# Cosine attention with a mixer behind it: the last score chunks of two head pairs in one score tile

## The chip, the core and the metric

The kernel runs on one core of a Trainium2 chip. The metric is device time in microseconds (us), the median of several executions; lower is better. The engines are TensorE (PE, with its weight loads shown as PEld), VectorE (DVE), ScalarE (ACT), GpSimd (POOL) and SyncE (SP). Each takes its instructions in the order in which they stand in its own queue. A fill of one engine by another is guarded by semaphores.

## What is computed

Inputs q, k and v have 8 batches, 12 heads, 448 rows and 64 columns. Each head's rows of q and k are normalised, the scores are divided by tau (0.1), and softmax and the product with v follow. The heads side by side give x with 448 rows and 768 columns for each batch, and a mixer follows:

```python
q_n = q / (np.linalg.norm(q, axis=-1, keepdims=True) + 1e-06)
k_n = k / (np.linalg.norm(k, axis=-1, keepdims=True) + 1e-06)
scores = np.matmul(q_n, k_n.transpose(0, 1, 3, 2)) / tau
attn = softmax(scores)                      # max subtracted, 1e-9 in the sum
x = heads side by side of np.matmul(attn, v)
h = x.transpose(0, 2, 1) @ U @ V            # rank 32 over the 448 rows
u = x + h.transpose(0, 2, 1)
out = u + np.maximum(u @ w_ch1, 0.0) @ w_ch2   # 768 -> 3072 -> 768
```

## The kernel before

Two heads make a pair, so each batch has six pairs, and all batches together have 48. For a pair, the keys of each head are cut into chunks of 128, 128, 128 and 64. Scores are held transposed: keys on the partitions, 448 queries on the columns. Chunks 0 to 2 take one score tile each (`sc`, two banks, one bank for each head), filled by four matmuls on the four 64x64 quarters of TensorE's array. The last chunk has 64 keys from each of the two heads, so both fit into the 128 partitions of one bank: one full 128x128 matmul, whose stationary side has zeros where a head has no keys, fills the first half of a score tile. There are two score tiles (tag `ps_sc`), used in turn. An exponential on ScalarE moves each tile into SBUF: 896 columns for chunks 0 to 2 (into `E`, one buffer for even and one for odd pairs), 448 columns for the last chunk (into `E3`, which has room for the two pairs of a couple: 0 and 1, 2 and 3, 4 and 5).

The product with v for a pair runs in two halves of the query rows. Each half begins with two matmuls that take the last chunk's exponentials as weights (line 376), and twelve for the other chunks follow (line 383). The first half goes to the bank `av`, the second to `mp`. VectorE divides each half by its sum (lines 394 and 395).

For batch 0 the order of everything is written out by hand as a list of words, `ORDER` (line 630). A word is put on its engine's queue when its turn comes, so the list is the order on each engine. The words that matter, with n a pair's number:

- `Tn`: TensorE transposes pair n's normalised q and k (bank `ps_x`, line 300). `Ten`: VectorE moves them into SBUF as `qkT` (line 305).
- `Snc`: the scores of chunk c of pair n (line 331, and line 324 for c = 3). `exnc`: their exponential (line 356, and line 353 for c = 3).
- `Vnh`: the product with v, half h. `Xnh`: VectorE's division.
- `An`: the product with U (line 416), into columns of bank `mp`. `Acn`: its copy into SBUF. `XTn`: the transpose of the divided result into `ps_x` (line 430). `Hn`: the product with V, added to it (line 441). `Un`: the move to `u` (line 446).
- `sc4q`, `sc4k` and their like: the scaling of q and k by their norms on POOL (.p) or VectorE (.v). `sq`, `red`, `root`, `inv`: the norms' squares, sums, roots and inverses. `val`: the values' cast. `l5q` and the like: loads on SP's queue. `w`n: matmuls of the identity without use, in the beginning. `w1_`i: a part of the first weight matrix, loaded by POOL's queue.
- `Mfab`: matmuls a to b of block f of the mixer's first product (line 655), which come when batch 0's `u` is nearly complete. `Rf`: their ReLU.

After the list, a loop goes over the pairs of the later batches and lays the mixer's matmuls of the batch before (lines 513 and 540) between the attention's steps. The second weight matrix comes in four transfers (line 173), all issued by POOL after squares and loads that stand ahead of them in its queue. A ReLU of the mixer's first product goes to ScalarE (line 517) or VectorE (line 519) by a planner's estimate: the object `est` keeps a running time for TensorE, ScalarE and VectorE, each step adds its estimated duration, and the engine that would be done first gets the work. In batch 0, too, the steps add their durations to it.

From pair 14 on the last chunks of two pairs are already handled together by `step_S3` (line 335): four matmuls on 64x64 quarters, the first pair's into the bank `av`, the second's into the bank `up`, and two exponentials.

Of the kernel before, what the change touches and what calls it, by code (L numbers as in the profile page):

```python
# [9 lines left out]
FP = mybir.dt.float32  # L10
BF = mybir.dt.bfloat16
AF = mybir.ActivationFunctionType
# [10 lines left out]
def kernel(  # L23
# [17 lines left out]
    nc = tc.nc  # L41

    B, H, S, D = q.shape
# [11 lines left out]
    psum = ctx.enter_context(tc.tile_pool(name="psum", bufs=1, space=bass.MemoryType.PSUM))  # L55
# [54 lines left out]
    E, E3 = [], []  # L110
# [37 lines left out]
    def place_v(copy, rows):  # L148
        lo = V_raw[rows, 0:256].rearrange("r (p c) -> r c p", c=4)
        hi = V_raw[rows, 256:448].rearrange("r (p c) -> r c p", c=3)  # L150
        body = V_sb[rows, 0:384].rearrange("r (c p) -> r c p", p=128)
        copy(out=body[:, :, 0:64], in_=lo[:, 0:3, :])
        copy(out=body[:, :, 64:128], in_=hi)
        copy(out=V_sb[rows, 384:448], in_=lo[:, 3, :])

    def place_u():
        nc.scalar.copy(out=U_sb[:, :, 0:R], in_=U_raw)
# [9 lines left out]
    def load_w1(f0, f1):  # L167
        nc.gpsimd.dma_start(out=w1_sb[:, :, f0:f1],
                            in_=moe_w_ch1[:, f0:f1].rearrange("(c p) f -> p c f", p=128))
# [20 lines left out]
    def load(gi, what, *engs):  # L190
        b, p0, n = groups[gi]
        engs = list(engs) * 4
        h0, nh = 2 * p0, 2 * n
        s = gi % NST

        def src(x, hs, lo, hi, c):
            return x[b, hs, lo:hi, :].rearrange("h (p c) d -> p h (c d)", c=c)

        def dst(t, ps, hs, c):
            return t[ps, hs, 0:c, :].rearrange("p h c d -> p h (c d)")  # L200

        L, U2 = slice(0, 64), slice(64, 128)
        if what == "q":
            allh = slice(h0, h0 + nh)
            engs[0].dma_start(out=dst(qst[s], L, slice(0, nh), 4), in_=src(q, allh, 0, 256, 4))
            engs[1].dma_start(out=dst(qst[s], U2, slice(0, nh), 3), in_=src(q, allh, 256, 448, 3))
            return
        x, t = (k, kst[s]) if what == "k" else (v, vst[s])
        m = min(3, nh)
        ou, mi = slice(h0, h0 + nh, 3), slice(h0 + 1, h0 + m)  # L210
        engs[0].dma_start(out=dst(t, L, slice(0, nh, 3), 4), in_=src(x, ou, 0, 256, 4))
        engs[1].dma_start(out=dst(t, U2, slice(0, nh, 3), 3), in_=src(x, ou, 256, 448, 3))
        engs[2].dma_start(out=dst(t, L, slice(1, m), 3), in_=src(x, mi, 0, 192, 3))
        engs[3].dma_start(out=dst(t, U2, slice(1, m), 4), in_=src(x, mi, 192, 448, 4))
# [89 lines left out]
    def evict_T(b, p):  # L304
        nc.vector.tensor_copy(out=new_qkT(b, p).rearrange("p a b -> p (a b)"),
                              in_=tp_of.pop((b, p)).rearrange("p a b -> p (a b)"))
        est.dve(0.69)
# [24 lines left out]
                                 rhs=t[r, 0, 0:S], start=True, stop=True)  # L332
        est.pe(0.25)

    def step_S3(b, p):

        for i, (nm, tag) in enumerate((("av", "ps_av"), ("up", "ps_x"))):
            t = qkT[(b, p + i)]
            bank = psum.tile([128, 512], FP, name=nm, tag=tag, bufs=1)
            sc_of[(b, p + i, 3)] = bank.unsqueeze(1)  # L340
            for h in range(2):
                r, o = slice(64 * h, 64 * h + 64), 64 * (h ^ i)
                nc.tensor.matmul(out=bank[o:o + 64, 0:S], lhsT=t[r, 1, 384 + o:448 + o],  # L343
                                 rhs=t[r, 0, 0:S], start=True, stop=True)
        est.pe(0.19)
        for i in range(2):
            exp_S(b, p + i, 3)

    def exp_S(b, p, c):
        e = E[(b * NP + p) % 2]  # L350
        sc = sc_of.pop((b, p, c))
        if c == 3:
            nc.scalar.activation(out=last_of(b, p)[:, 0:S], in_=sc[:, 0, 0:S], func=AF.Exp)  # L353
            est.act(0.56)
        else:
            nc.scalar.activation(out=e[:, 2 * c:2 * c + 2, 0:S], in_=sc[:, :, 0:S], func=AF.Exp)  # L356
            est.act(0.93)
# [62 lines left out]
    def evict_A(b, p, copy):  # L420
        A_of[(b, p)] = A_sb[p % 2]
        copy(out=A_sb[p % 2][0:64, :], in_=av_of[(b, p, 1)][0:64, 384:512])
# [17 lines left out]
    def pe_H(b, p):  # L440
        nc.tensor.matmul(out=up_of[(b, p)], lhsT=A_of[(b, p)], rhs=V_sb,  # L441
                         start=False, stop=True, skip_group_check=True)
        est.pe(0.19)
# [143 lines left out]
    pairs = [(b, p) for b in range(B) for p in range(NP)]  # L587
# [33 lines left out]
    def Hs(n):  # L621
# [11 lines left out]
        red2q ex02 S03 w6 ex03 val0 l3v T1 root2 val1 l4q l4k l4v V00 Te1 plU inv2 S10 V01  # L633
        sc2q.v S11 ex10 w9 sc2k.v ex11 X01 sc3k.p S12 T2 X00 ex12 S13 sc3q.p Te2 A0 w3 sq3q.a plV.p
        Ac0.v S20 T3 sq3k.a w19 red3q ex13 red3k ex20 S21 V10 ex21 w1_0 V11 X10 S22 Te3 root3 val2
        l5q l5k l5v S23 ex22 inv3 XT0 H0 X11 sc4q.p ex23 S30 U0.v ex30 V20 sc4k.v S31 A1 ex31 S32
        X20 sc5q.p T4 Ac1.v ex32 Te4 V21 sc5k.p S33 X21 XT1 ex33 S40 val3 H1 ex40 A2 U1.v S41 V30
        Ac2.v ex41 S42 X30 T5 ex42 V31 Te5 S43 X31 ex43 S50 XT2 ex50 A3 S51 Ac3.v H2 V40 ex51 U2.v
        S52 X40 V41 w1_1 ex52 S53 X41 XT3 sq4q ex53 H3 A4 U3.a V50 Ac4.v XT4 X50 V51 sq4k H4 U4.a X51
        M004 A5 red4q Ac5.a XT5 M104 H5 U5.a M045 M145 M205 red4k root4 M056 M156 R0 inv4 sc6q.v sc6k.v  # L640
        R1 M256 M306 R2 R3
    """
# [2 lines left out]
    copies = {"a": nc.scalar.copy, "v": nc.vector.tensor_copy}  # L645
    QK = {"q": 0, "k": 1}

    opened = {}

    def pe_m1(fb, lo, hi):  # L650
        if lo == 0 and fb % 2 == 0:
            t = psum.tile([128, 2, 512], FP, name="sc", tag="ps_sc", bufs=2)
            opened[fb], opened[fb + 1] = t[:, 0, 0:S], t[:, 1, 0:S]
        for cc in range(lo, hi):
            nc.tensor.matmul(out=opened[fb], lhsT=w1_sb[:, cc, fb * 128:(fb + 1) * 128],
                             rhs=uE[:, cc, 0:S], start=(cc == 0), stop=(cc == CC - 1),
                             skip_group_check=True)

    def evict_m1(fb):
        nc.scalar.activation(out=relu[:, fb, 64:64 + S], in_=opened.pop(fb), func=AF.Relu)  # L660

    def word(w):
        w, _, eng = w.partition(".")
        if w.startswith("w1_"):
            i = int(w[3:])
            load_w1(768 * i, 768 * (i + 1))
        elif w[0] == "w":
            for _ in range(int(w[1:])):
                nc.tensor.matmul(out=spare[:, 0:128], lhsT=ident, rhs=ident, start=True, stop=True)
        elif w[0] == "l":  # L670
            load(int(w[1]), w[2], nc.sync)
        elif w == "plU":
            place_u()
        elif w == "plV":
            place_v({"a": nc.scalar.copy, "p": nc.gpsimd.tensor_copy}[eng], slice(0, R))
        elif w[0] == "M":
            pe_m1(int(w[1]), int(w[2]), int(w[3]))
        elif w[0] == "R":
            evict_m1(int(w[1]))
        elif w.startswith("sq"):  # L680
            preps[int(w[2])].square(QK[w[3]], eng == "a")
        elif w.startswith("red"):
            preps[int(w[3])].reduce(QK[w[4]])
        elif w.startswith("root"):
            preps[int(w[4])].root()
        elif w.startswith("inv"):
            preps[int(w[3])].invert()
        elif w.startswith("val"):
            preps[int(w[3])].values()
        elif w.startswith("sc"):  # L690
            gi, j = group_of[pairs[int(w[2])]]
            preps[gi].scale(QK[w[3]], j, {"v": V_, "p": P_}[eng])
        elif w.startswith("Te"):
            evict_T(*pairs[int(w[2])])
        elif w.startswith("ex"):
            exp_S(*pairs[int(w[2])], int(w[3]))
        elif w.startswith("XT"):
            pe_XT(*pairs[int(w[2])])
        elif w.startswith("Ac"):
            evict_A(*pairs[int(w[2])], copies[eng])  # L700
        else:
            at = pairs[int(w[1])]
            if w[0] == "T":
                pe_T(*at)
            elif w[0] == "S":
                pe_S(*at, int(w[2]))
            elif w[0] == "V":
                half = int(w[2])
                pe_V(*at, half, bank1 if half else
                     psum.tile([128, 512], FP, name="av", tag="ps_av", bufs=1))  # L710
            elif w[0] == "X":
                divide_V(*at, int(w[2]))
            elif w[0] == "A":
                pe_A(*at)
            elif w[0] == "H":
                pe_H(*at)
            else:
                assert w[0] == "U", w
                evict_H(*at, copies[eng])
# [78 lines left out]
    for n in range(NP, NPAIR + 1):  # L798
        b, p = pairs[n] if n < NPAIR else (B, 0)
# [116 lines left out]
```

## Time and profile before

| What | Value |
|---|---|
| median of 10 executions | 579.9 us (579.54 to 581.8) |
| the profiled execution's own time | 580.26 us |
| its span in the profile | 578.5 us |
| TensorE busy | 568.6 us, 98% of the span |
| ScalarE busy | 262.2 us, 45% |
| VectorE busy | 212.2 us, 37% |
| POOL busy | 213.8 us, 37% |
| granted TensorE clock | 1.00 |

The part that the change touches lies between about 24 and 36 us of the span. The table by stretches (start and end, length, then the busy time and number of instructions of PE, PEld, DVE, ACT and POOL, the granted clock, the DMA engines' busy share and GB/s) shows how the engines are taken up around it:

```profile
20.00:25.00 5.00, 4.60 (x76) 3.41 (x76) 4.40 (x9) 4.39 (x8) 2.85 (x5) 1.00 0.84 165
25.00:30.00 5.00, 4.93 (x75) 3.12 (x74) 4.12 (x12) 4.45 (x7) 3.53 (x3) 1.00 1.15 229
30.00:35.00 5.00, 4.90 (x83) 3.31 (x83) 3.55 (x11) 4.57 (x6) 2.77 (x3) 1.00 1.16 247
35.00:40.00 5.00, 4.84 (x74) 3.59 (x73) 3.92 (x10) 2.57 (x5) 2.85 (x2) 1.00 1.10 209
40.00:45.00 5.00, 5.00 (x28) 2.61 (x27) 4.10 (x7) 3.58 (x8) 1.85 (x2) 1.00 1.12 258
```

Here three engines are taken up nearly all the time between 20 and 35 us, TensorE, ScalarE and VectorE, and from 40 us on TensorE has no hole in a stretch. A matmul's busy time includes its way through the array, so that a matmul's length is more than what it holds the engine; the distance from its start to the next one's is what it holds.

### The profile page before, as it was taken

The numbers are of one execution on the slowest core, as the hardware profiler recorded it, in microseconds if no ns is written. First come the engines' busy times: TensorE is split into PE (matmuls) and PEld (weight loads), VectorE is DVE, ScalarE is ACT, GpSimd is POOL, SyncE is SP. The second block draws the span as 40 slices with busy tenths as digits, with TensorE's granted clock in tenths as the row PEclk, the third lists the DMA queues.
The fourth block names the chain that finished last, engine by engine and source line by source line (L and its number), as shares of the span: only waits on it lengthen the run. The fifth ranks groups of instructions, "written<-read, shape, count | busy, mean of one in ns | idle before, by whom it ended". The sixth has DMA issues, their size and how long they took to land.

```text
span 578.5 us, 12301 instructions
## 1 busy us (share of the span) xinstructions
PE 568.6 (98%) x5098; PEld 329.2 (57%) x5098; DVE 212.2 (37%) x460; ACT 262.2 (45%) x449; POOL 213.8 (37%) x202
## 2 busy tenths in 40 slices
PE   7899999999999999999999999999999999999997
PEld 6665566555565556555555555655565545555565
DVE  7874551433342334423324343432244332320011
ACT  5877544455333653446324555246443374214300
POOL 8756564715416236416055064253261420000000
PEclk9999999999999999999999999999999999999999
DMA  6899999696477376575365663773755640231022
GB/s 163 192 236 238 236 210 211 168 170 139 101 151 164 88 146 127 132 153 109 87 158 147 119 137 97 149 174 80 132 129 115 133 74 14 56 69 37 5 50 57
DMA packets 139881, 74.52 MB, mean 129 GB/s; under 512 B 86688, under 2 KB 139696, under 8 KB 139824
## 3 DMA queue, kind: packets, MB, share of 16 engines
q1 hardware_dynamic: 129568, 63.20, 50.7%
q0 software_dynamic: 9632, 10.01, 10.2%
q8 instruction: 40, 0.66, 0.5%
q10 hardware_dynamic: 624, 0.51, 0.3%
q14 instruction: 17, 0.14, 0.1%
HBM read 52.19 MB, written 11.01 MB: 109 GB/s over the span
## 4 chain that ended last, share of the span: by engine, by line
PE 86%; DMA 8%; DVE 1%; ACT 1%; SPq 1%; POOL 1%; issue 1%; ACTq 0%; DVEq 0%; POOLq 0%
PE mp L540 38%; PE mp L513 33%; DMA w_sb<-in_moe_w_ch_dram 5%; PE sc L331 5%; PE av L383 3%; PE up L383 2%; DMA qst<-in_q_dram 2%; DMA kst<-in_k_dram 2%; PE av L343 1%; PE av L376 1%; PE up L376 1%; PE up L469 1%; PE av L483 1%; ACT E L356 0%; DVE qk L268 0%
## 5 line engine op out<-in xcount | busy, mean ns | idle before, releaser
L540 PE MATMUL mp<-w_sb,relu 128*128 128x384 bf16 (+2 forms) x1368 | 233.6, 323 | 0.6 <-DMA w_sb<-in_moe_w_ch_dram 0.6
L540 PEld LDWEIGHTS <-relu 128*128 128x128 bf16 x1368 | 126.8, 98 | 89.0 <-issue 13.8
L513 PEld LDWEIGHTS <-w_sb 128*128 128x128 bf16 x1128 | 105.1, 98 | 99.1 <-issue 9.3
L517 ACT ACTIVATE relu<-mp 128x448 bf16<-128x448 f32 x163 | 88.7, 544 | 128.2 <-PE mp L513 128.2
L356 ACT ACTIVATE E<-sc 128x896 bf16<-128x896 f32 x144 | 125.2, 922 | 22.4 <-PE sc L331 21.4
L268 POOL TENSOR_TENSOR qk<-kst,inv 128x512 bf16<-128x512 f32 x43 | 45.9, 1068 | 234.6 <-DVE inv L262 227.5
L513 PE MATMUL mp<-uO,w_sb 128*128 128x448 bf16 x576 | 114.2, 352 | 0.0
L513 PE MATMUL mp<-uE,w_sb 128*128 128x448 bf16 x552 | 112.9, 353 | 0.0
L558 DVE TENSOR_TENSOR o_sb<-mp,ut 128x384 f32<-128x384 f32 (+2 forms) x51 | 28.0, 550 | 141.0 <-PE mp L540 141.0
L248 DVE TENSOR_REDUCE ss<-sq 128x16 f32<-128x1024 f32 (+1 forms) x50 | 57.7, 1165 | 1.6 <-POOL sq L243 0.8
L268 POOL TENSOR_TENSOR qk<-qst,inv 128x512 bf16<-128x512 f32 x44 | 47.4, 1077 | 1.3 <-PE up L441 1.3
L383 PEld LDWEIGHTS <-E 128*128 128x128 bf16 x1152 | 45.0, 97 | 0.0
L519 DVE TENSOR_SCALAR relu<-mp 128x448 bf16<-128x448 f32 x25 | 15.6, 625 | 76.3 <-PE mp L513 75.8
L331 PE MATMUL sc<-qkT 64*64 64x448 bf16 x576 | 42.3, 359 | 0.6 <-ACT E L356 0.3
L243 POOL TENSOR_TENSOR sq<-kst 128x1024 f32<-128x1024 f32 (+1 forms) x23 | 42.6, 1855 | 0.2
L243 POOL TENSOR_TENSOR sq<-qst 128x1024 f32<-128x1024 f32 x21 | 39.7, 1890 | 7.4 <-DMA qst<-in_q_dram 6.7
L276 POOL CAST v<-vst 128x1024 bf16<-128x1024 f32 (+1 forms) x25 | 25.1, 1004 | 15.6 <-DMA vst<-in_v_dram 13.1
L353 ACT ACTIVATE E<-av 128x448 bf16<-128x448 f32 x17 | 9.2, 540 | 47.3 <-PE up L343 47.3
L383 PE MATMUL av<-v,E 128*128 128x65 bf16 x624 | 28.0, 193 | 0.0
L394 DVE RECIPROCAL rd<-av 128x4 f32<-128x4 f32 x52 | 9.3, 179 | 47.3 <-PE av L383 47.3
L473 ACT CAST A_sb<-up 128x128 bf16<-128x128 f32 x19 | 5.0, 264 | 47.6 <-PE up L469 47.6
L376 PEld LDWEIGHTS <-E 128*128 128x128 bf16 x192 | 18.0, 98 | 14.5 <-issue 0.8
(97 smaller groups left out, 347.8 us busy)
## 6 DMA issues: line engine op xcount, KB each, us to landing
out_dram<-o_sb SPq DMA_DIRECT2D x108, 96.0 KB, 2.2
w_sb<-in_moe_w_ch_dram POOLq DMA_DIRECT2D x8, 1152.0 KB, 18.3
qst<-in_q_dram SPq DMA_DIRECT2D x23, 256.0 KB, 3.9
vst<-in_v_dram SPq DMA_DIRECT2D x46, 128.0 KB, 3.1
kst<-in_k_dram SPq DMA_DIRECT2D x44, 128.0 KB, 2.8
qst<-in_q_dram SPq DMA_DIRECT2D x23, 192.0 KB, 4.0
vst<-in_v_dram SPq DMA_DIRECT2D x46, 96.0 KB, 2.8
kst<-in_k_dram SPq DMA_DIRECT2D x44, 96.0 KB, 2.7
```

Source lines behind the costliest of these rows:

```text
L243: nc.gpsimd.tensor_mul(sq[:, 0:self.nh * 4, :], self.flat(t), self.flat(t))
L248: nc.vector.reduce_sum(self.ss[:, j, 0:self.nh * 4], self.sq[j][:, 0:self.nh * 4, :], axis=AX.X)
L268: eng.tensor_mul(qks[self.gi % 2][:, j, i, :, :, :], t[:, 2 * j:2 * j + 2, :, :].rearrange("p h c d -> p c h d"), iv.unsqueeze(3).to_broad ...
L276: nc.gpsimd.tensor_copy(out=self.flat(v65[self.s])[:, :, 0:D], in_=self.flat(vst[self.s]))
L331: nc.tensor.matmul(out=sc[o:o + 64, h, 0:S], lhsT=t[r, 1, c * 128 + o:c * 128 + o + 64], rhs=t[r, 0, 0:S], start=True, stop=True)
L356: nc.scalar.activation(out=e[:, 2 * c:2 * c + 2, 0:S], in_=sc[:, :, 0:S], func=AF.Exp)
L376: nc.tensor.matmul(out=av[:, i, :, :], lhsT=last_of(b, p)[:, ic * 128:(ic + 1) * 128], rhs=vv[:, 2 * j:2 * j + 2, 3, :], start=(i == 0), s ...
L383: nc.tensor.matmul(out=av[:, i, h, :], lhsT=e[:, 2 * c + h, ic * 128:(ic + 1) * 128], rhs=vv[:, 2 * j + h, c, :], start=False, stop=(i == ...
L513: nc.tensor.matmul(out=mp, lhsT=w1_sb[:, cc, f * 128:(f + 1) * 128], rhs=u[:, cc, 0:S], start=(cc == 0), stop=(cc == CC - 1))
L517: nc.scalar.activation(out=relu[:, f, o:o + S], in_=mp, func=AF.Relu)
L540: nc.tensor.matmul(out=mp, lhsT=relu[:, f, r0:r0 + 128], rhs=w2_sb[:, f, half * HC + c0:half * HC + c1], start=(f == 0), stop=(b > 0 and f ...
L558: nc.vector.tensor_add(o.rearrange("p (k d) -> p k d", d=128), mp.rearrange("p (k d) -> p k d", d=128), ut_of[(b, half)][:, c0 // 128:c1 / ...
```

## The change

In batch 0 the last chunks of pairs 2 and 3, and of pairs 4 and 5, are computed together. The words `S23`, `ex23`, `S33`, `ex33`, `S43`, `ex43`, `S53`, `ex53` go. The words `Q2`, `exQ2`, `Q4` and `exQ4` come. `Q`n takes one score tile, fills one bank for each of the two pairs with two 64x64 matmuls each, and `exQ`n is one exponential of 896 columns for both pairs, straight into the couple's `E3`. Pairs 0 and 1 stay as they were. The first score chunk of the couple's second pair (`S30`, `S50`) moves ahead of `Q`, since `Q` needs the transposed tiles of both pairs; in the second couple `S51` and its exponential stand where they did. The function that issues the matmuls is split off from `step_S3`, which the later batches go on using as before. `Q` adds 0.19 to TensorE's estimate, as `step_S3` does; `exQ` adds nothing to ScalarE's.

```diff
-    def step_S3(b, p):
-
-        for i, (nm, tag) in enumerate((("av", "ps_av"), ("up", "ps_x"))):
+    def pe_S3(b, p, banks):
+
+        for i, bank in enumerate(banks):
             t = qkT[(b, p + i)]
-            bank = psum.tile([128, 512], FP, name=nm, tag=tag, bufs=1)
             sc_of[(b, p + i, 3)] = bank.unsqueeze(1)
             for h in range(2):
                 r, o = slice(64 * h, 64 * h + 64), 64 * (h ^ i)
                 nc.tensor.matmul(out=bank[o:o + 64, 0:S], lhsT=t[r, 1, 384 + o:448 + o],
                                  rhs=t[r, 0, 0:S], start=True, stop=True)
         est.pe(0.19)
+
+    def step_S3(b, p):
+        pe_S3(b, p, [psum.tile([128, 512], FP, name=nm, tag=tag, bufs=1)
+                     for nm, tag in (("av", "ps_av"), ("up", "ps_x"))])
         for i in range(2):
             exp_S(b, p + i, 3)
...
-        l5q l5k l5v S23 ex22 inv3 XT0 H0 X11 sc4q.p ex23 S30 U0.v ex30 V20 sc4k.v S31 A1 ex31 S32
-        X20 sc5q.p T4 Ac1.v ex32 Te4 V21 sc5k.p S33 X21 XT1 ex33 S40 val3 H1 ex40 A2 U1.v S41 V30
-        Ac2.v ex41 S42 X30 T5 ex42 V31 Te5 S43 X31 ex43 S50 XT2 ex50 A3 S51 Ac3.v H2 V40 ex51 U2.v
-        S52 X40 V41 w1_1 ex52 S53 X41 XT3 sq4q ex53 H3 A4 U3.a V50 Ac4.v XT4 X50 V51 sq4k H4 U4.a X51
+        l5q l5k l5v S30 ex22 inv3 XT0 H0 X11 sc4q.p ex30 Q2 U0.v exQ2 V20 sc4k.v S31 A1 ex31 S32
+        X20 sc5q.p T4 Ac1.v ex32 Te4 V21 sc5k.p S40 X21 XT1 val3 H1 ex40 A2 U1.v S41 V30
+        Ac2.v ex41 S42 X30 T5 ex42 V31 Te5 S50 X31 XT2 ex50 A3 Q4 Ac3.v H2 exQ4 S51 V40 U2.v ex51
+        S52 X40 V41 w1_1 ex52 X41 XT3 sq4q H3 A4 U3.a V50 Ac4.v XT4 X50 V51 sq4k H4 U4.a X51
...
-    opened = {}
+    opened, couple_of = {}, {}
...
+        if w[0] == "Q":
+            both = psum.tile([128, 2, 512], FP, name="sc", tag="ps_sc", bufs=2)
+            couple_of[w[1]] = both
+            pe_S3(*pairs[int(w[1])], [both[:, 0, :], both[:, 1, :]])
+        elif w.startswith("exQ"):
+            nc.scalar.activation(out=E3[int(w[3]) // 2 % 2][:, :, 0:S],
+                                 in_=couple_of.pop(w[3])[:, :, 0:S], func=AF.Exp)
+        elif w.startswith("w1_"):
```

More of the change, by code (lines that the diff above doesn't have):

```diff
@@ L663, in word @@
         w, _, eng = w.partition(".")
-        if w.startswith("w1_"):
+        if w[0] == "Q":
[6 more added lines that the diff above has]
+        elif w.startswith("w1_"):
             i = int(w[3:])
```

## The prediction

> **What bounds the kernel now.** First the page: TensorE (PE) is busy 98% of the span, so the time is TensorE's work plus its holes. Then the waits of TensorE after 40 us, to see whether it has holes there at all (columns: who waited for whom, total us, times, longest).
>
> ```profile
> span 578.5 us, 12301 instructions
> PE 568.6 (98%) x5098; PEld 329.2 (57%) x5098; DVE 212.2 (37%) x460; ACT 262.2 (45%) x449; POOL 213.8 (37%) x202
> ...
> PE mp L540 <- DMA w_sb<-in_moe_w_ch_dram: 0.6, 1, 0.6
> ```
>
> There is one, 0.57 us, for a transfer of the second weight matrix. The chain of waits shows what this transfer hangs on (start, length, what):
>
> ```profile
> 47.46 1.89 POOL sq L243
> 49.35 0.82 POOL w_sb L168
> 50.17 1.00 POOL w_sb L173
> 51.17 28.46 DMA w_sb<-in_moe_w_ch_dram
> ...
> 79.67 1.14 PE mp L540 x6
> ```
>
> POOL issues it at 51.17, after squares that waited for loads, and it lands at 79.6. No step of the attention's TensorE work is in this chain. So a microsecond that TensorE gains before 79 us is waited away here, and of a microsecond lost before, 0.57 comes back. From 79.67 on the chain is TensorE until the end: what arrives late there is late for good.
>
> Now the stretch of the change, TensorE and ScalarE (ACT) by the timeline (start, length, engine, line, operation, out<-in, count):
>
> ```profile
> 24.05 0.38 PE L331 MATMUL sc<-qkT 64*64 64x448 bf16 x4
> 24.37 0.36 PE L324 MATMUL sc<-qkT 128*128 128x448 bf16 x1
> 24.96 0.36 PE L430 MATMUL up<-ident,X 128*128 128x128 bf16 x4 [0.23 <-DVE qkT L305]
> 25.16 0.35 PE L441 MATMUL up<-V_sb,A_sb 128*128 128x448 bf16 x1
> 25.46 0.38 PE L331 MATMUL sc<-qkT 64*64 64x448 bf16 x4
> 25.90 0.29 PE L376 MATMUL av<-v,E 128*128 128x130 bf16 x2
> 26.03 0.54 PE L383 MATMUL av<-v,E 128*128 128x65 bf16 x12
> 26.50 0.38 PE L331 MATMUL sc<-qkT 64*64 64x448 bf16 x4
> ```
> ```profile
> 24.49 0.92 ACT L356 ACTIVATE E<-sc 128x896 bf16<-128x896 f32 x1
> 25.30 0.54 ACT L353 ACTIVATE E<-sc 128x448 bf16<-128x448 f32 x1
> 25.89 2.77 ACT L356 ACTIVATE E<-sc 128x896 bf16<-128x896 f32 x3
> ```
>
> The first list reads S22, S23, XT0, H0, S30, V20 (two lines), S31. V20 starts at 25.90, 0.06 after ex23 ends (25.30 + 0.54): its first weights are the last chunk's exponentials, and S31 stands behind it on an in-order engine. ScalarE goes from ex23 straight on.
>
> **Rules for the replay, from these rows.** A score group holds TensorE 0.31 before other work (24.05 to 24.37), an entry from full-size work costs 0.10 more (H0 to S30 takes 0.30, H0 to the next full-size matmul 0.20), the full-size S23 0.19, a half of V 0.60 before scores and 0.50 before full-size work, XT and H 0.20 each. A score group is complete 0.38 after its start; ScalarE starts some 0.05 later; TensorE restarts 0.06 after what it waited for. An exponential of 896 columns lasts 0.92, the next may start 0.09 before its end.
>
> **The gain in itself.** Four full-size score matmuls go (4 x 0.19 = 0.76 of TensorE) and two groups of four 64x64 matmuls come (2 x 0.31, entry 2 x 0.10): 0.82, a loss of 0.06. On ScalarE 4 x 0.54 = 2.16 go and 2 x 0.92 = 1.84 come, 0.32 less. That is an upper bound of what the merging can give, and ScalarE is not the end of the chain here.
>
> A note on Q's own cost: its four matmuls write two banks, and in each bank both row halves of the array write. The nearest row is the same arrangement in later batches, complete in 0.38, with the next scores 0.21 after its start:
>
> ```profile
> 122.46 0.38 PE L343 MATMUL av<-qkT 64*64 64x448 bf16 x2
> 122.47 0.38 PE L343 MATMUL up<-qkT 64*64 64x448 bf16 x2
> 122.68 0.55 PE L331 MATMUL sc<-qkT 64*64 64x448 bf16 x8
> ```
>
> I take 0.38. The Trainium skill, "TensorEngine Tiling (Array Packing)", Gotcha 1: PSUM Pressure, speaks against it: it says that different row tiles can't use one PSUM bank at the same time. By that rule each Q would run as two turns and end about 0.19 later, and the sum below would be 0.4 higher; the rows above decide against it.
>
> **First couple, step by step.** S30 takes S23's place, but reads pair 3's transposed tile, whose eviction on VectorE ends at 24.91 (XT0 waited for it too): S30 at 24.97, ready 25.35. ex30 25.40 to 26.32. XT0 25.28, H0 25.48, Q2 25.78 (its score tile is free since ex22 ended at 25.41), ready 26.16. exQ2 26.23 to 27.15. V20 waits for it: 27.21 instead of 25.90, **+1.31**. TensorE stands for 1.1 us there, and S31, A1, S32 and T4 behind it move by the same; ScalarE, having done ex30 and exQ2, has nothing from 27.15 to 28.24, when S31's scores come (27.81 + 0.38 + 0.05). T4 28.76 instead of 27.45; V21 29.22, as it waits only for VectorE's copy of A1 (28.83); the eviction of T4 ends at 30.11. S33 no longer stands between, so S40 waits for that eviction alone: 30.17 instead of 29.14, +1.03. XT1, which stood ahead of S40, now stands behind it (0.20): S41 31.20 instead of 29.98, +1.22. V30 31.51, S42 32.11, T5 32.42, its eviction 33.08 to 33.77, S50 33.83 instead of 32.61: **+1.22**.
>
> **Second couple.** XT2 34.14, A3 34.38 (pair 3's second division on VectorE ends at 34.32), Q4 34.70, ready 35.08, H2 35.01, S51 35.31. On ScalarE ex50 34.26 to 35.18, exQ4 35.09 to 36.01, so V40 36.07. Before, V40 started 1.37 after S50 (32.61 to 33.98), now 2.24 after: **+2.09**. S52 36.67, V41 36.98 instead of 34.89. S53 and ex53 are gone from the end, but the step there is set by V41, its division on VectorE, and A4:
>
> ```profile
> 36.29 0.38 PE L416 MATMUL mp<-X,U_sb 128*128 128x128 bf16 x4 [0.16 <-DVE X L395]
> ```
>
> A4 waited 0.16 for that division, so what S53 frees (0.19) is waited away. A4 38.38, +2.09. From here TensorE's order is dense in both kernels.
>
> **The rest.** Of 2.09, 0.57 come back at the weight transfer: 1.52. The moves of VectorE's reductions for group 4 (38.46 to 40.8, now 2.1 later) stay ahead of the square at 45.58 that reuses their tiles, and the loads on SP's queue and the weight loads on POOL's wait for none of the moved steps until 55 us; if they did move along, the 0.57 would not come back. The planner's books: the new words charge 2 x 0.19 to TensorE and nothing to ScalarE, where 4 x 0.30 and 4 x 0.56 stood. The order of instructions shows one effect: the first ReLU that VectorE took (53.48 us, 0.62) goes to ScalarE, after the two small activations that end at 54.37. Then the exponential at 55.06 starts at 55.28, and V of the next batch's first pair (56.16) would wait until 55.28 + 0.92 + 0.06 = 56.26: 0.1. Bounds 0 (if the other ReLU takes up the shift) and 0.25 (all of it); I take 0.1. All other engines' orders stay as they were.
>
> Sum: -0.57 + 2.09 + 0.1 = +1.6 us. The profiled execution took 580.26 (span 578.5 and 1.8 around it), which gives 581.9; it lies 0.36 above the median of 579.9, and the median becomes 581.5. The replay's restarts are good to some 0.05 each, eight of them in a row: 0.4 either way, so 581.1 to 581.9 for this case.
>
> **Rivals.**
> (1) The loss is larger. The weight transfer lands later along with TensorE, so that 0.57 isn't recovered, or Q's halves take turns: +2.1 to 2.3, 582.1. Against it: the chain above and the row of 0.38. For it: DMA is busy at 1.1 of 16 engines' time in this stretch, so a shifted load may push the transfer.
> (2) Not slower: TensorE does not stand behind exQ2. Either S31 gets past V20, or exQ2 is done sooner than I think, so that the merged exponential's 0.32 on ScalarE counts. Decides: V20 before 26.5, or V41 before 36.6 (1.7 late, of which 1.16 are left at the end). If the loss at V41 is 0.57 or less, the transfer's wait takes all of it and the time stays 579.9; half way, 580.5. For it: ScalarE is busy 4.4 to 4.6 of 5 us from 20 to 35, and has one exponential less at the end of the stretch. Against it: V20's weight load waited for ex23 in the profile, and S31 came only after V20.
> (3) Faster: the same, and the whole stretch shrinks, so that the transfer lands sooner too. ScalarE's 0.32 and the two small waits of ScalarE for S33 and S53 (0.23 and 0.24) bound it: 579.1, if the transfer moved by as much. Nothing in the chain says that it would.
>
> **Chances.** Forecast 0.60, rival (1) 0.12, rival (2) 0.23, rival (3) 0.05. 0.2% is 1.16 us, about what a measurement of this kernel tells from no change: slower by more 0.72 (forecast and (1)), within 0.23, faster 0.05. The range goes from 580.3, which takes in half of (2), to 582.3, the upper end of (1).
>
> **What would show it.** In the profile after: V20's first matmuls (two of 128x130 into av) start near 27.2 and wait for ScalarE's merged exponential, TensorE idle about 1.1 us before; ScalarE idle about 1.1 us near 27.2; V40 near 36.1, with 0.4 of TensorE idle before it; A4 near 38.4; TensorE's wait for the weight transfer near 79.6 gone. I am wrong if V20 starts before 26.5, if A4 is less than 1.7 us late, or if the transfer's wait stays.

## The result, and the profile after

The changed kernel takes 583.2 us in the median (581.27 to 583.41), the kernel before 580.0 in the runs beside it: a ratio of 1.004 (95% interval 1.0029 to 1.005), 2.3 us slower by this ratio and 3.2 by the medians. The forecast was slower, 581.5, range 580.3 to 582.3. So the direction was right and the size was not.

The single executions say more than the median. Five of ten lie at 581.3 to 581.7, five at 583.2 to 583.4, nothing between, and the mean granted clock (0.999 or 1.000) does not tell them apart. The forecast describes the lower level; the upper one was not foreseen. The median is that of the nine executions beside the profiled one, five of them upper; with a share of about one half it could as well have come out at the lower level. The profile at hand is of the lower level: 581.64 us against 580.26 of the profiled execution before.

The page of the changed kernel, its span, TensorE's busy time and the chain that ended last by engine:

```profile
span 579.9 us, 12307 instructions
...
PE 567.6 (98%) x5102; PEld 328.3 (57%) x5102; DVE 211.4 (36%) x459; ACT 262.1 (45%) x448; POOL 213.6 (37%) x202
...
PE 95%; ACT 1%; DVE 1%; SPq 1%; DMA 1%; issue 0%; DVEq 0%; ACTq 0%
```

TensorE works 1.0 us less than before, in a span 1.4 us longer. The transfer of the second weight matrix, 5% of the chain before, is gone from it, and among TensorE's waits after 40 us there is no row left. The timeline of TensorE shows where the time went (line numbers are 3 higher than before; L342 is Q, L379 the first two matmuls of V):

```profile
24.97 0.38 PE L331 MATMUL sc<-qkT 64*64 64x448 bf16 x4 [0.53 <-DVE qkT L305]
...
25.78 0.38 PE L342 MATMUL sc<-qkT 64*64 64x448 bf16 x4
27.19 0.29 PE L379 MATMUL av<-v,E 128*128 128x130 bf16 x2 [1.03 <-ACT E L672]
...
34.68 0.38 PE L342 MATMUL sc<-qkT 64*64 64x448 bf16 x4
34.99 0.36 PE L444 MATMUL up<-V_sb,A_sb 128*128 128x448 bf16 x1
...
36.09 0.29 PE L379 MATMUL av<-v,E 128*128 128x130 bf16 x2 [0.42 <-ACT E L672]
...
38.41 0.38 PE L419 MATMUL mp<-X,U_sb 128*128 128x128 bf16 x4 [0.35 <-DVE X L398]
```

The lines are S30, Q2, V20, Q4, H2, V40 and A4. V20 stands 1.03 us for the merged exponential (L672) and V40 0.42. ScalarE stands in turn, since the next scores are queued behind V:

```profile
24.50 1.82 ACT L359 ACTIVATE E<-sc 128x896 bf16<-128x896 f32 x2
26.22 0.91 ACT L672 ACTIVATE E<-sc 128x896 bf16<-128x896 f32 x1
28.22 1.73 ACT L359 ACTIVATE E<-sc 128x896 bf16<-128x896 f32 x2 [1.09 <-PE sc L331]
```

Replay and trace side by side, start in us:

| step | before | forecast | after |
|---|---|---|---|
| Q2 | - | 25.78 | 25.78 |
| V20 | 25.90 | 27.21 | 27.19 |
| S41 | 29.98 | 31.20 | 31.18 |
| S50 | 32.61 | 33.83 | 33.82 |
| V40 | 33.98 | 36.07 | 36.09 |
| A4 | 36.29 | 38.38 | 38.41 |

### The profile page after: what moved, and what is told of

It reads as the page before. It is cut to its first block, busy times and chain, and to the rows that moved or that the text cites. A ratio compares the mean times of both kernels' runs of the same rounds, so it can differ in the third digit from the quotient of the medians.

```text
span 579.9 us, 12307 instructions
## 1 busy us (share of the span) xinstructions
PE 567.6 (98%) x5102; PEld 328.3 (57%) x5102; DVE 211.4 (36%) x459; ACT 262.1 (45%) x448; POOL 213.6 (37%) x202
## 4 chain that ended last, share of the span: by engine, by line
PE 95%; ACT 1%; DVE 1%; SPq 1%; DMA 1%; issue 0%; DVEq 0%; ACTq 0%
PE mp L543 38%; PE mp L516 37%; PE sc L331 6%; PE av L386 3%; PE up L386 2%; PE av L379 1%; PE av L342 1%; PE tp L300 1%; PE sc L658 1%; ACT E L359 1%; PE up L379 1%; PE up L472 1%; DMA qst<-in_q_dram 1%; PE av L486 1%; DVE qkT L305 0%
## 5 line engine op out<-in xcount | busy, mean ns | idle before, releaser
L379 PEld LDWEIGHTS <-E 128*128 128x128 bf16 x192 | 17.9, 98 | 16.1 <-ACT E L672 2.0
```

The source lines that it names most:

```text
L379: nc.tensor.matmul(out=av[:, i, :, :], lhsT=last_of(b, p)[:, ic * 128:(ic + 1) * 128], rhs=vv[:, 2 * j:2 * j + 2, 3, :], start=(i == 0), s ...
```

## The experiments

All comparisons are with the kernel before, run beside them on the same chip.

**again: the changed kernel once more, for a profile of the upper level.**

> The changed kernel again, to see its two levels of time (581.3 to 581.7 in half of its executions, 583.2 to 583.4 in the other half) and, with luck, a profile of the upper one. Theory G (the TensorE clock): TensorE stands for 1.0 us before V20 and for 0.3 to 0.5 us in three more places, and in some executions the granted clock falls for a few us after it. An upper profile then shows a stretch with a granted clock near 0.5 after 27 us and everything behind it 1.6 us later. Theory D (transfers): the clock stays at 1.00 and the upper profile shows TensorE waiting some 1.6 us for a transfer that the lower one does not wait for, the second weight matrix first of all. Theory S (the start): the upper profile is late by 1.6 us already before 24 us, by the first loads. Times: two levels again, 581.5 and 583.3.

Six executions: 581.41, 581.60, then 583.31 to 583.72 three times and 584.27. The profile is of the upper level (583.39 us, clock 1.000); of the other three upper executions one, too, has a clock of 1.000, and 583.72 and 584.27 have 0.997. At 40 us it is 0.13 us behind the other profile. The timeline of TensorE, VectorE (DVE) and POOL in this upper execution, three fences:

```profile
47.56 0.61 PE L300 MATMUL tp<-ident,qk 128*128 128x128 bf16 x8
48.01 1.30 PE L516 MATMUL mp<-uE,w_sb 128*128 128x448 bf16 x6
50.84 0.57 PE L331 MATMUL sc<-qkT 64*64 64x448 bf16 x8 [1.54 <-DVE qkT L305]
```
```profile
44.30 0.69 DVE L268 TENSOR_TENSOR qk<-qst,inv 128x512 bf16<-128x512 f32 x1
44.91 2.38 DVE L268 TENSOR_TENSOR qk<-kst,inv 128x512 bf16<-128x512 f32 x1
47.21 2.38 DVE L268 TENSOR_TENSOR qk<-qst,inv 128x512 bf16<-128x512 f32 x1
49.51 0.68 DVE L268 TENSOR_TENSOR qk<-kst,inv 128x512 bf16<-128x512 f32 x1
50.11 0.68 DVE L305 COPY qkT<-tp 128x1024 bf16<-128x1024 bf16 x1
```
```profile
44.74 2.00 POOL L243 TENSOR_TENSOR sq<-qst 128x1024 f32<-128x1024 f32 x1 [1.92 <-DMA qst<-in_q_dram]
46.70 2.34 POOL L243 TENSOR_TENSOR sq<-kst 128x1024 f32<-128x1024 f32 x1
```

Nobody hands anything to anybody between these two groups. VectorE scales q and k of batch 1's first pairs, POOL squares those of the group after. Yet two of the four scalings last 2.38 us instead of 0.69, and each ends 0.55 us after the square that was running (46.74 and 49.04; 47.29 and 49.59): VectorE stood until POOL's square was done, and then did its own work. The eviction of the transposed tile, queued behind them, ends at 50.79, and TensorE waits 1.54 us for it. In the profile of the lower level the load for the square landed later:

```profile
44.16 0.69 DVE L268 TENSOR_TENSOR qk<-qst,inv 128x512 bf16<-128x512 f32 x1
...
45.98 0.69 DVE L268 TENSOR_TENSOR qk<-kst,inv 128x512 bf16<-128x512 f32 x1
```
```profile
46.89 1.88 POOL L243 TENSOR_TENSOR sq<-qst 128x1024 f32<-128x1024 f32 x1 [3.28 <-DMA qst<-in_q_dram]
```

There the last scaling was over 0.22 us before the square began. Before the change the scalings ran from 42.32 to 44.83, and the square began at 45.58:

```profile
44.14 0.69 DVE L268 TENSOR_TENSOR qk<-kst,inv 128x512 bf16<-128x512 f32 x1
```
```profile
45.58 1.88 POOL L243 TENSOR_TENSOR sq<-qst 128x1024 f32<-128x1024 f32 x1 [2.90 <-DMA qst<-in_q_dram]
```

TensorE's S of the next batch starts 1.74 us later in the upper profile than in the lower (50.84 and 49.10), the times differ by 1.75; 0.13 of it was there at 40 us. For this execution all three theories of the expectation fall as they stood: the clock was full, TensorE waited for no transfer, and the start was not late. What differs between the two profiles is the moment at which a load lands, and it acts by way of POOL. Why the load lands at another time is not shown.

**first_only and second_only: one couple merged.** The edit puts the words of the other couple back as they were.

> Only pairs 2 and 3 are merged; 4 and 5 as before. The replay says: V20 at 27.2, S50 1.22 us late, A4 1.22 us late, of which 0.57 are given back at the weight transfer: +0.65 us, 580.7 at the lower level. Theory G: the long stand before V20 is still there, so the upper level stays, at 582.3 (in something like half of the executions). Theories D and S have no reason why the levels should depend on which couple is merged: D has it grow with the lateness, so fewer upper executions than with both couples; S the same share.

> Only pairs 4 and 5 are merged; 2 and 3 as before. The replay says: V40 0.87 us late (34.85), A4 0.87 us late, 0.57 given back: +0.3 us, 580.3 at the lower level. Theory G: the longest stand left is 0.4 us, so no upper level, or a rare one. Theory S: the same share of upper executions as with both couples.

The second couple alone: nine of eleven executions at 580.10 to 580.47, median 580.33 (1.0006, 0.9997 to 1.0014), where the replay said 580.3; two at 581.0 with a clock of 0.997, by the one profiled of them a fall of the clock at 8 to 14 us, before the change. The first couple alone (median 581.62; 1.0031, 1.0016 to 1.0045): six of twelve at 580.70 to 580.97 (replay: 580.7), one at 582.27, five at 583.25 to 583.52, and these five all have a clock of 0.996. Its profile is one of them. The table by stretches (behind the busy times and counts of the five engines: granted clock, DMA share, GB/s):

```profile
24.00:28.00 4.00, 2.45 (x37) 1.31 (x35) 3.12 (x9) 3.01 (x5) 2.46 (x2) 0.95 1.11 209
28.00:32.00 4.00, 4.00 (x45) 2.69 (x42) 2.08 (x6) 2.22 (x3) 2.95 (x4) 0.63 1.13 262
```

After the stand of 1.03 us the granted clock fell (0.63 from 28 to 32 us; in the profile of both couples 1.00 there), the replay's A4 at 37.5 became 38.56, and then two scalings of 2.38 us follow as in again. So in this execution there is a second cause, the fall of the clock of theory G, which makes TensorE about 1.1 us late and thereby brings on the first.

**dense_delay and dense_hold: the lateness without the merging.** dense_delay is the kernel before with useless matmuls ahead of V20; dense_hold adds the hold described next.

```diff
-        ... sc4q.p ex23 S30 U0.v ex30 V20 sc4k.v S31
+        ... sc4q.p ex23 S30 U0.v ex30 w37 V20 sc4k.v S31
```

> The kernel before with 37 matmuls of the identity without use put ahead of V20: TensorE is 2.1 us later from there on, as with the change, but works all that time. The replay says A4 2.1 us late and +1.5 us, 581.5, and TensorE's wait for the weight transfer gone. Theory G: no stand, so one level only, near 581.5. Theory D: the lateness is the same as with the change, so the same two levels, 581.5 and 583.1.

> The kernel before, delayed by 37 matmuls of the identity ahead of V20 as in dense_delay, with the same hold of POOL's squares. Nothing of the merging is in it. Theory P: the upper level that the delay alone brought (583.0 to 583.3) is gone, one level at 581.4 to 581.9. Rival L: two levels stay. Rival W: one level with a wait near 80 us.

TensorE worked where the change makes it stand, A4 came at 38.16 (1.87 late), and the two levels were there: 581.4 and 581.9, and three of five at 582.99 to 583.34, all at a clock of 0.999 or more (ratio 1.0049, 1.0036 to 1.0063). With the hold, eleven of eleven at 581.16 to 581.86 (1.0024, 1.0015 to 1.0033). The two intervals don't meet. Neither the merged exponential nor the stand is needed for the upper level; lateness alone brings it, and with the hold it is gone.

The profile of dense_delay is of its lower level (581.40 us), and yet one scaling was caught (VectorE, POOL and TensorE):

```profile
45.73 2.38 DVE L268 TENSOR_TENSOR qk<-kst,inv 128x512 bf16<-128x512 f32 x1
48.03 0.68 DVE L305 COPY qkT<-tp 128x1024 bf16<-128x1024 bf16 x1
```
```profile
45.30 2.26 POOL L243 TENSOR_TENSOR sq<-qst 128x1024 f32<-128x1024 f32 x1 [2.14 <-DVE qk L268]
47.52 2.34 POOL L243 TENSOR_TENSOR sq<-kst 128x1024 f32<-128x1024 f32 x1
```
```profile
48.85 0.57 PE L331 MATMUL sc<-qkT 64*64 64x448 bf16 x8
```

The eviction was done at 48.71, and TensorE started the scores at 48.85 without a wait. So one scaling behind one square still fits into the slack; the upper profile has two. The kernel before may not be free of this either: ten of its 108 executions beside all these runs lie at 581.0 to 582.3, the others at 579.2 to 580.7. None of the ten was profiled, and their cause stays open.

**hold and hold_fill: scalings and squares kept apart.** POOL copies one column of VectorE's last scaling into a tile of its own (`gate`) before it squares; hold_fill fills the stands, too.

```diff
+        if gi == 5:
+            put(*at[0], lambda: nc.gpsimd.tensor_copy(out=gate, in_=qks[0][:, 1, 1, 3, 1, 0:1]))
         put(*at[0], lambda g=g: g.square(0))
# hold_fill besides:
-        ... ex30 Q2 U0.v exQ2 V20      ... exQ4 S51 V40
+        ... ex30 Q2 w16 U0.v exQ2 V20  ... exQ4 S51 w6 V40
```

> The changed kernel, and POOL copies one column of VectorE's last scaling of group 4 before it starts the squares of group 5, so that the two never run side by side. Theory P (the upper level of 583.3 is VectorE's four scalings, now 2.1 us later, running into POOL's two squares, two of them 2.38 us instead of 0.69): the upper level is gone and all executions at full clock lie at 581.3 to 581.9. Rival L (late loads make the upper level, the slow scalings only go with it): two levels as before, half of the executions near 583.3. Rival W (holding the squares moves the second weight matrix's transfers, issued behind them, by up to 2 us): one level, but with a new wait of TensorE near 80 us, up to 583.

> As hold, and TensorE's two stands are filled with matmuls of the identity without use (16 ahead of V20, 1.0 us; 6 ahead of V40, 0.4 us). Theory G2 (a second, rarer cause: after the stand of 1.0 us the granted clock falls to about a half for some 3 us, as in the profile with the first couple alone): no execution below a clock of 0.999 that the kernel before does not have too, one level at 581.3 to 581.9. If the clock's fall has nothing to do with the stand, executions at 0.996 to 0.997 stay.

hold: 581.39 to 581.78 four times, and 582.53 and 583.06 with clocks of 0.997 and 0.996; in first_only the fall of the clock alone made TensorE 1.1 us late. hold_fill: seven of seven at 581.33 to 582.08, no clock below 0.999. The medians are 581.75 (1.0033, 1.002 to 1.0045) and 581.61 (1.0027, 1.0016 to 1.0038); six and seven executions are few, and these intervals touch that of the changed kernel, so the verdict rests on the levels. In hold's profile the four scalings last 0.69 us each and the square waits for them:

```profile
46.08 0.69 DVE L269 TENSOR_TENSOR qk<-kst,inv 128x512 bf16<-128x512 f32 x1
```
```profile
46.84 0.18 POOL L768 CAST gate<-qk 128x1 f32<-128x1 bf16 x1 [3.91 <-DVE qk L269]
46.98 1.88 POOL L244 TENSOR_TENSOR sq<-qst 128x1024 f32<-128x1024 f32 x1
```

Counting only executions at a clock of 0.999 or more: without the hold (the changed kernel twice, dense_delay) 10 of 19 lie above 582.9, with it (hold, hold_fill, dense_hold) 0 of 22. Theory P stands; L falls, as loads were not touched; W falls, as no wait near 80 us appeared. That the clock's fall comes from the stand is likely but less sure: below 0.998 were 9 of 34 executions with the stand of 1 us open (changed kernel twice, first_only, hold), none of 34 where it was filled, cut to 0.2 us, or replaced by work (hold_fill, qfirst, dense_delay, dense_hold). But there are also two of eleven of second_only, in another place, and, in the last three runs, on another chip, one each of the 11, 11 and 12 of w2early, tuned_plain and tuned (the latter two with the stand cut to 0.2 us, too) and three of 29 of the kernel before, which has none in its 47 executions beside the other runs.

**qfirst: Q ahead of the second pair's first scores.**

```diff
-        S30 ex22 inv3 XT0 H0 X11 sc4q.p ex30 Q2 U0.v exQ2 V20
+        Q2 ex22 inv3 XT0 H0 X11 sc4q.p exQ2 S30 U0.v ex30 V20
-        S50 X31 XT2 ex50 A3 Q4 Ac3.v H2 exQ4 S51 V40
+        Q4 X31 XT2 exQ4 A3 S50 Ac3.v H2 ex50 S51 V40
```

> The changed kernel with Q ahead of the second pair's first scores (Q2, exQ2 ahead of S30, ex30; Q4, exQ4 ahead of S50, ex50), so that V waits for one exponential less. The replay: Q2 24.97, exQ2 done at 26.3, V20 26.4 (+0.5 instead of +1.3), V40 34.7 and A4 37.0 (+0.7 instead of +2.1), of which 0.57 are given back: 580.1 at the lower level. Theory P: VectorE's scalings end near 45.5 instead of 46.7, the squares of POOL begin at 44.3 to 46.9, so fewer executions at the upper level of 583.3 than with the change, not none. If V20's wait is not what costs, 581.5 stays.

V20 at 26.39 after a stand of 0.21, V40 at 34.80, A4 at 37.11 (+0.8). Eleven executions at 580.00 to 580.89, median 580.39 (1.0008, 0.9999 to 1.0016), none at the upper level. The wait of V for one exponential more was the main loss of the lower level: without it A4 is 1.3 us less late.

**w2early, tuned_plain, tuned: can it beat the kernel before?** w2early moves the weight transfers ahead of the squares on POOL; tuned_plain moves T4, T5 and three matmuls of M004 forward in qfirst; tuned does both.

> The kernel before, with POOL issuing the last part of the first weight matrix and the first two transfers of the second weight matrix right after the third part, ahead of the squares of group 5 (at about 42.7 to 46.5 instead of 49.3 to 52.2). The attention's steps are as before. Theory of the prediction (before, TensorE stands at 79 us for this transfer, and only this hides lateness or swallows a gain): the wait is gone, 0.6 to 0.7 us less than before, 579.0. Rival: the transfers are bound by the DMA engines' total work, so the wait stays or moves to the queries' and keys' loads of group 5: the same time or more.

> As qfirst, with three moves on TensorE: T4 ahead of S32 and T5 ahead of S42, so that the transposed tiles are evicted before S40 and Q4 want them, and three of the four matmuls of M004 put ahead of A4, where TensorE stood 0.34 us. The replay: A4's successors some 0.7 us earlier than in qfirst, about as late as in the kernel before. By the theory the wait for the second weight matrix then is back, 0.5 to 0.7 us, and the time is that of the kernel before, 579.6 to 580.0, or 0.4 less than qfirst. If a gain before 79 us counts in full, 579.6 or less without that wait.

> tuned_plain with the transfers of w2early. If both theories hold, the wait is gone and TensorE is dense from the same point as before: 579.0, 0.6 less than the kernel before and no slower than w2early by more than 0.3. If the merged chunks are worth something in themselves once V doesn't wait for them, it is faster than w2early; if not, the same or slower.

None beats it: w2early 580.11 (1.0001, 0.9992 to 1.001), tuned_plain 580.17 (1.0007, 0.9999 to 1.0016) and tuned 580.14 (1.0013, 0.9996 to 1.0031). w2early shows in its chain of waits why an earlier issue gains nothing:

```profile
43.86 1.00 POOL w_sb L173
44.86 34.77 DMA w_sb<-in_moe_w_ch_dram
...
79.68 1.14 PE mp L540 x6
```

Issued 6.3 us earlier (44.86 instead of 51.17), the transfer landed at the same 79.6. The issue does not set the landing. The rival's reason, the DMA engines' total work, fits, as the engines moved 235 GB/s from 40 to 79.5 us in the profile before and 234 in w2early, with a busy share of 1.19 in both; no run tests it alone. tuned_plain's profile is of its slowest execution (581.88). TensorE reached that point at 79.46, 0.3 us earlier than in qfirst, which had no wait there, and stood:

```profile
81.16 1.14 PE L543 MATMUL mp<-w_sb,relu 128*128 128x384 bf16 x6 [1.54 <-DMA w_sb<-in_moe_w_ch_dram]
```

The transfer landed 1.5 us later than in the profiles of the kernel before and of w2early. The engines moved only 228 GB/s from 40 to 79.5 us here; the 0.28 MB that are missing against the kernel before would take 1.2 us at that rate, an estimate that fits the rival's reason. Why they moved less is not shown, nor whether the wait came back in the faster executions. tuned is at 579.68 to 580.38 in nine executions, and at 582.26, 582.90 and 585.72 in three; in the profiled one (582.90) a scaling of 4.97 us stood behind both squares, and TensorE waited 2.90 us for the eviction after it:

```profile
44.72 4.97 DVE L268 TENSOR_TENSOR qk<-kst,inv 128x512 bf16<-128x512 f32 x1
```
```profile
45.36 1.93 POOL L243 TENSOR_TENSOR sq<-qst 128x1024 f32<-128x1024 f32 x1
47.22 1.91 POOL L243 TENSOR_TENSOR sq<-kst 128x1024 f32<-128x1024 f32 x1
```

## Why the prediction was right and wrong

1. *V20 waits behind exQ2, +1.31; S50 +1.22; V40 +2.09; A4 +2.09.* Right to 0.03 us at each step (table above), and qfirst, first_only and second_only moved by what the same rules say.
2. *Q's own cost, 0.38.* Right: both Q last 0.38 in the profile. As ends of matmuls are modelled there, the starts say more: H2 follows Q4 by 0.31 (34.68 to 34.99), just as other work follows an ordinary score group. The Trainium skill's page "TensorEngine Tiling (Array Packing)", Gotcha 1: PSUM Pressure, says that different row tiles can't use one PSUM bank at the same time. Two turns by that rule would have made H2 0.19 later, an estimate; no such delay is in these rows.
3. *0.57 come back at the weight transfer.* Right in kind: the wait is gone. In size it was 0.73: the matmuls ahead of it in the profile before started at 78.74 and hold TensorE 0.20, so it stood from 78.94 to 79.67; the 0.57 count from the modelled end.

```profile
78.74 0.36 PE L430 MATMUL up<-ident,X 128*128 128x128 bf16 x4
79.67 1.14 PE L540 MATMUL mp<-w_sb,relu 128*128 128x384 bf16 x6 [0.57 <-DMA w_sb<-in_moe_w_ch_dram]
```

4. *The ReLU that changes engine, +0.1.* Wrong, 0. The ReLU did go to ScalarE, but the exponential behind it starts 2.18 later than before (57.24 instead of 55.06), where the forecast had 0.22 on top of the 2.09. V of the next batch's first pair starts at 58.28, 2.12 after its 56.16 before, just as late as the steps ahead of it (40.01 instead of 37.89).
5. *Sum +1.6.* Between the two profiled executions it is 1.38, which is 2.12 less 0.73, so the two terms above account for the difference; the lower level of 581.3 to 581.7 holds the forecast of 581.5.
6. *"The moves of VectorE's reductions for group 4 ... stay ahead of the square at 45.58 that reuses their tiles", and "from here TensorE's order is dense in both kernels".* The first holds: the reductions end at 43, and the square begins at 44.7 or later. The second is the step that failed, and with it the loss between there and the weight transfer, put at nothing. I followed the lateness to the next handover of data and found cover there, but not on to the scalings behind the reductions. They were 0.75 us clear of POOL's squares before; 1.8 to 2.0 us later, they are clear only when the load for the square lands late enough, and these scalings and squares stand in each other's way though they hand each other nothing: 2.38 us instead of 0.69 for two scalings, and a wait of 1.54 us for TensorE. About half of the executions pay some 1.7 us for it, and the median of the changed kernel happened to fall into that half. Rival (1) had a larger loss, but by other mechanisms: neither the transfer's landing nor turns in Q. That the lower level holds the 581.5 is no luck, as the steps up to A4 came as foretold; that the median lies at the upper level is partly chance.
7. The clock's fall after the stand was not in the forecast either. In the ten executions of the result it plays no part (0.999 to 1.000), in first_only it does.
8. Rival (3) names the two small waits of ScalarE as those for S33 and S53; the second (0.24) is for S43, as the wait stands ahead of the exponential at 32.55. No sum rests on the name.

The Trainium skill has such a mechanism: "SBUF — State Buffer", section Who interferes with whom, says that a VectorE instruction with two inputs in SBUF contends with a GpSimd instruction that reads SBUF, that the ports they share are an exclusive lock, and that the order of issue decides who is blocked. The scalings have two such inputs and the squares read SBUF; the rows of again agree, 2.38 us being the rest of a square and the scaling's own time. The row of tuned doesn't fit as well: that scaling starts 0.64 us ahead of the first square and still ends 0.56 us after the second. Which port it is no run here shows.

## What to carry to other kernels

When a step gets later, carry the lateness through every engine, also past the next handover of data, and ask what will then run beside what; a margin of 0.75 us between VectorE and POOL is a resource like a buffer. Merging two small operations makes the consumer of the first wait for the producer of both, so place the merged one ahead of work that nobody waits for yet, and look for a later fixed point (here a transfer at 79.6 us) that swallows a gain. Look at single executions, not only the median: a change that moved work close to such an edge showed here as two levels.

## What was not expected of the hardware

A stand of TensorE of 1.03 us between busy stretches was followed, in the profiled execution of first_only, by a granted clock of 0.63 over the next four microseconds, with the matmuls of the transposes at 1.03 instead of 0.62 us for eight; after the same stand in the profiles of the result, again and hold the clock stayed at 1.00. And a transfer issued 6.3 us earlier landed at the same time, 79.6 us, with the DMA engines' busy share at 1.1 to 1.3 all that while.
